# One GpSimd power for the RMS root, block 0 started by four heads, and a new written order: sliding-window attention with a SwiGLU feed-forward on one Trainium2 core

## The chip, the cores and the metric

The kernel runs on one core of a Trainium2 chip. The metric is the time of one execution on the device in microseconds (us); lower is better. A core has TensorE (PE, matmuls; PEld is its weight load), VectorE (DVE), ScalarE (ACT), GpSimd (POOL) and SyncE (SP). SP and ACT issue DMAs through hardware queues, POOL through a software queue. The eight banks of PSUM take what PE writes.

## What is computed

Four sequences of 768 tokens with 8 heads of 64 go through causal attention with a window of 128 keys and 4 sink keys that every query sees; then an RMS norm; then a SwiGLU feed-forward of 512 to 1536 to 512:

```python
keep = is_sink | ((rel >= 0) & (rel < 128))
scores = np.where(keep, q @ k.T / sqrt(64), -1e9)
a = softmax(scores); x = a @ v                       # 3072 rows of 512
xn = x / np.sqrt(np.mean(x * x, -1) + 1e-6) * rms_g
g = xn @ w_gate
out = (g * sigmoid(g) * (xn @ w_val)) @ w_out
```

## The kernel before

**Blocks and groups.** The 3072 rows are 24 blocks of 128 tokens, numbered 0 to 23, six to a sequence. The feed-forward takes groups of four blocks (512 rows), numbered 0 to 5.

**One block of attention.** q, k and v of a block are loaded (`load_bf16` L351, `load_v` L355, by POOL, which casts to bf16; each is one DMA of 256 KB read). Only q and k of block 0 come as fp32 through SP (`load_f32` L343) and are cast by ACT or DVE (`cast` L347). q and k are transposed: up to block 7 by PE and a copy out of PSUM (`pe_t` L441, `copy_t` L450), from block 8 on by a DMA on SP (`dma_t` L457). Keys stand on the partitions: the scores of a key block hold its own queries and the next block's (`scores` L474; `tri_scores` L551 leaves out the masked triangle; `scores_last` L492). In blocks 0 and 1 the mask is a matmul ahead of the scores (`mask_bias` L464); later masks are multiplied by DVE or selected by POOL (`tri_pool` L590). ACT takes exponentials. `av` (L602) multiplies by v, which has a column of ones for the denominators, in two halves of four heads. `normal` (L655, DVE) divides. `square` (L666, ACT) sums the squares of a row. `rms` (L674, DVE) adds 1e-6, takes the reciprocal root by a start from the bits and a polynomial, six one-column instructions, and multiplies the row by root and gain `gb` (L693). The result xr is transposed into xnt, by PE for blocks 0 to 7 (`pe_x`, `copy_x`), by a DMA on SP from block 8 on (`dma_x` L719).

**The feed-forward.** `mms` (L971) makes gate (g) and value (v) sums, 16 matmuls of 128x128 to a bank in group 0, 8 of 128x256 in groups 1 and 2, 4 of 128x512 later; `tanh`, `silu`, `hidden` (ACT, DVE, DVE) make hT; `project` (L1004) takes four matmuls of 128x512 at a time; ACT evacuates and SP stores.

**What sets the order.** Nothing is scheduled when the program is built. The kernel lists its steps (1077 before) with what each needs and gives, and `Plan.run` replays them in an order that is written out: for each engine a list of step numbers (`ORDER`), the interleaving of the engines (`TURNS`) and the PSUM banks (`BANKS`). Names like LOAD_LEAD, T_LEAD, GATE_FROM only add to the needs that `Plan.run` asserts; they put no wait into the program. Each engine runs its list strictly in order; waits come from the data. A load on POOL also waits for the landing of the load eight before it.

In what follows sN are the scores of block N, avN its two products with v, qN, kN, vN its loads or transposes, msN the sum of squares. Before, POOL's list begins (after each name, its place among the loads where it matters): q1, identity, bias, k1, v0, wg columns 0-1 (4th), q2, q3, v1, k2, wg 2-3 (9th), k3, wv 0-1 (11th), wv 2-3 (12th), v2, wg 4-5, wg 6-7, wv 6-7, wv 4-5, wg 8, 9, 10-11 (18th to 20th), wv 8, 10-11, 9 (21st to 23rd), q4, v3, k4, q5, q6, wo first half, k5, v4, wo second half, q7, v8, q8, v5, k6, k7, k8, v6, v7, q9, k9, v9, q10, k10, v10, q11, k11, v11, and so on by blocks.

SP's list has after the first loads: the transposes q8, q9, k8, k9, q10, one store, q11, k10, k11, q12, q13, k12, ...

Of the kernel before, what the change touches and what calls it, by code (L numbers as in the profile page):

```python
# [9 lines left out]
ALU = mybir.AluOpType  # L10
# [5 lines left out]
P = 128  # L16
# [3 lines left out]
C3 = -5.0 / 16.0  # L20
T1 = 2.5258847276
TP = T1 - 4.2
TQ = 7.0 / T1
# [66 lines left out]
""",  # L90
    "ACT": """
24 20 22 199 177 175 178 176 182 180 181 183 168 188 222 204-206 211 207 212 209 191 210
217 226 228 227 229 195 598 220 236 603 613 618 608 243 633 628 260 623 245 247 246 248
638 278 262 255 264-267 197 280 282 284 653 273 320 648 643 295 297 659 290 322 299 301
300 302 276 324 325 293 326 327 309 664 678 669 683 674 333 312 693 340 316 341 688 342
343 698 355-357 336 358 703 370 371 708 372 318 373 349 385 364 387 718 713 723 739 379
399 401 400 402 728 418 419 733 420 393 421 409 763 758 778 768 754 773 744 749 427 433
414 783 434-436 448 449 793 450 798 451 442 808 788 819 803 463-466 813 457 824 480 475
482 494 496 497 495 513 488 514 515 504 834 838 516 848 843 853 829 863 868 858 878 873
525 883 531-533 893 509 888 534 899 923 549-551 928 552 938 543 567-569 918 570 585 587  # L100
933 943 948 561 953 579 958 909 904 968 593 963 914 973 1008 1003 994 998 1013 1028 1023
989 1038 1018 1033 984 1053 1048 1043 979 1069 1059 1064 1072 1073
""",
    "DVE": """
# [13 lines left out]
""",  # L118
    "POOL": """
25 8 9 26-28 31 34 30 32 37 35 29 38 33 39 41 42 40 43 45 47 44 48 46 49 36 50 53 57 52  # L120
54 51 56 63 62 60 55 58 64 61 59 65-99 467 469 468 470 481 100 483 101-108 517 520 109
518 519 535 538 537 536 110 553 555 554 571 573 556 572 588 586 574
""",
    "SP": """
# [7 lines left out]
ASDDSDGDPDPSPDPPPPPGPPPGPDPGPPDDPGAGPPPPADGPPPPGPPSPDPSADPGSDPSPGAAAPAGPAPPDAPPGPPAPDPAP  # L132
PPPADPGPDAGPPDPPDGAPPGPAPPAGDPAPAPDGADAPDGPAPPPADPAGPDAPADAGPPPPAPADGAPADGPPPPPAPPDPGPPD
DPAGPDPAGPDPGAPDDGPDGPDADGDPDGPADADPGAADPGPGDPADGAPDPGADAPGADADPGDPAPPDAPPDADAPGDPPADAGP
AAGPAPDAPPDPADPDAPGDAPDDGDPAPGDPPGSAAPGADAPGDPDGPPPDAGDAPGDADPPGADPAGDSAPPAGASPADPADSADP
PPGADAPGPSADDPGASAPGDPGSAPPGDPSADGAPDASDAPPDADPAGPPSAAADPAADPADPDAPAGADPGADPPDAPPADDPDGS
PDAPASAGDPPAPAGDSPADAPADDPPAGSADPPDASDPAGPADPSDDPGAPDDPADAPDGSDPDGPAGAPADSAPPADSDPPDGPDS
PDAGASPAAPDASGDPADSPDSDPGSPPPDDPSDGPDADPAPADPSDPSPDPSPDDAPDPDAPADPADAPDADAPDPDPASAPDASAP
DSADPADPDPASAPASADPAPPDASDPDAPSDASPADPDADPDPDPDAPASAPPDASADPAGPDGPGDPDGAPDPDPDPDAPAAGPSA
DGPAASGPADSPAGDPPGDDPGPPDGPDAAGPPDAGADPAGPAAGDPADAGPGPDSPGDPDASGPDGAADSPDAPDSDPPDSPDAPDS  # L140
ADPDSAPPDSDPSDAPDASPADDPDPDPADAPAAPDASADPADSPGSDGPDGSPGPGPAPAPADPAPDADPADAPDAGAPDGPGPAAP
AAPPADGDPPDGPDGDGPPAAPDSPGDPGAGPDAPPDPDPDPDAADPADPDDPAPAADPSDPDPDDPAAPPSPDDPAAPDPPSPPDPA
PSDSDSPASDPDPPPAAPDDPDPDPPAAPSDPDPAPDDPDPPPPAAPDADPSDPAAPDPDPAAPDDPDPDAPADPDPDPDPPDPAAPD
SPSDPPPPPAAPSASSPAADS
"""
BANKS = """
0123456701234567012345645645635654353513714370432704614654154761061305147237235720165760
7615743764051726351402376152376015237653746573746574631547613547647136210735462047136524
7012473650241762350741602735410721356421305406354063420675134632745013274350174362507431
6542371607152374153275461237104573604156324175032407615342047562310462317460170414217326  # L150
5047314243270172316412040572153042573045
# [4 lines left out]
def kernel(  # L156
# [35 lines left out]
    F32_LOADS = ("ks0","qs0")  # L192
    GROW = "SP"
    CAST_DVE = 600
# [10 lines left out]
    GATE_FROM = 8  # L205
    LOAD_LEAD = 10
    LEAD_FROM = 10
    WARM = 56
    GATE_LEAD = 14
    T_LEAD = 4  # L210
# [9 lines left out]
    ld = ctx.enter_context(tc.tile_pool(name="ld", bufs=LD))  # L220
# [59 lines left out]
    dve(150, lambda: nc.vector.memset(ones, 1.0), gives=["ones"], prio=-96)  # L280
    if WARM:
        zeros = const.tile([P, P], BF16, name="zeros")
        dve(70, lambda: nc.vector.memset(zeros, 0.0), gives=["zeros"], prio=-99.6)
# [50 lines left out]
    for i in range(NS):  # L334
        sp(430, 2600, lambda i=i: load_sink(i), ["vsink1", "grow"], [("vsink", i)], -70 + i)
# [7 lines left out]
    def load_f32(name, src, g, eng):  # L343
        T["st", name, g] = opool.tile([P, H, D], FP32, name="stage", tag="osb")
        eng.dma_start(out=T["st", name, g], in_=block_of(src, g))

    def cast(name, g, copy):  # L347
        T[name, g] = ld.tile([P, H, D], BF16, name=name)
        copy(out=T[name, g], in_=T.pop(("st", name, g)))

    def load_bf16(name, src, g):  # L351
        T[name, g] = ld.tile([P, H, D], BF16, name=name)
        nc.gpsimd.dma_start(out=T[name, g], in_=block_of(src, g))  # L353
# [76 lines left out]
    def scale_gb():  # L430
        nc.scalar.mul(gb, BANK.pop(("gb",)), C3)
# [709 lines left out]
```

## Time and profile before

| | |
|---|---|
| three runs | 241.31, 242.18, 242.49 us |
| median | 242.18 us |
| profiled execution: span from its first to its last instruction | 241.9 us |
| TensorE clock granted | 1.00 throughout |
| ACT busy, POOL busy | 122.8, 89.2 us |
| software queue (q0): packets, share of the time of 16 DMA engines | 81760, 79.3% |

The profile is one execution; it has no time of its own beside its span, which lies 0.28 us under the median of the runs. A page's row of a group gives line, engine, operation, output and inputs, count, then busy time, mean of one in ns, and idle time before with what ended it. In a row of the timeline the first number is the start in us, the second the duration in us, and the brackets give the idle time ahead and its releaser.

### The profile page before, as it was taken

Reading aid. Unit: us, or ns where it says so; the run is one execution under the profiler, and the core shown is the slowest. Engines: PE = TensorE matmul, PEld = TensorE weight load, DVE = VectorE, ACT = ScalarE, POOL = GpSimd, SP = SyncE. Lnnn points to the kernel's source line nnn. Section 1 sums busy time; section 2 is a strip of 40 time slices with the busy share of each in tenths; the row PEclk is TensorE's granted clock in tenths of the full one; section 3 lists DMA queues with packets and bytes.
Section 4 is the critical chain, followed back from the end, with each engine's and each line's share of the span. In section 5 each row is a group of like instructions: output and inputs, shape, how many; then the busy total and the mean of one; then the engine's idle time right before and its main releaser. Section 6 shows DMA issues by size and latency. Waiting matters only on the chain.

```text
span 241.9 us, 5897 instructions
## 1 busy us (share of the span) xinstructions
PE 231.3 (96%) x2329; PEld 147.6 (61%) x2354; DVE 187.4 (77%) x478; ACT 122.8 (51%) x267; POOL 89.2 (37%) x116
## 2 busy tenths in 40 slices
PE   7889999999879999999999999999999999999995
PEld 5568986876668776777876644445554444444443
DVE  3599989989979999999898989994569946537520
ACT  4776368667766574337654464454543321233112
POOL 8985894597526554000004982022540000000000
PEclk9999999999999999999999999999999999999999
DMA  9999999999999999999601999527010114101024
GB/s 128 143 183 195 182 178 194 162 143 139 137 151 152 138 143 154 132 233 156 126 2 24 119 150 123 131 70 128 3 23 0 32 36 173 43 0 47 0 87 173
DMA packets 113741, 27.42 MB, mean 113 GB/s; under 512 B 103857, under 2 KB 110769, under 8 KB 113714
## 3 DMA queue, kind: packets, MB, share of 16 engines
q0 software_dynamic: 81760, 13.90, 79.3%
q1 hardware_dynamic: 31810, 12.95, 29.8%
q8 instruction: 18, 0.29, 0.5%
q10 hardware_dynamic: 144, 0.20, 0.2%
q14 instruction: 9, 0.07, 0.1%
HBM read 28.35 MB, written 6.29 MB: 143 GB/s over the span
## 4 chain that ended last, share of the span: by engine, by line
PE 67%; DMA 20%; POOL 6%; issue 2%; DVE 2%; SPq 2%; POOLq 0%
PE v L975 20%; PE o L1008 20%; PE g L975 18%; DMA wo<-in_moe_w_out_dram 5%; DMA qkT<-q 4%; DMA wv<-in_moe_w_val_dram 4%; DMA wg<-in_moe_w_gate_dram 3%; DMA q<-in_q_dram 3%; POOL v L357 2%; SPq L459 2%; PE s L563 2%; PE av L621 2%; POOL k L353 1%; PE av L616 1%; PE o_last L1028 1%
## 5 line engine op out<-in xcount | busy, mean ns | idle before, releaser
L975 PE MATMUL v<-xnt,wv 128*128 128x128 bf16 (+2 forms) x527 | 72.2, 282 | 0.4 <-DMA wv<-in_moe_w_val_dram 0.2
L975 PE MATMUL g<-xnt,wg 128*128 128x128 bf16 (+2 forms) x521 | 71.3, 281 | 0.4
L1008 PE MATMUL o<-wo,hT 128*128 128x512 bf16 x259 | 65.3, 379 | 1.1 <-issue 0.5
L982 ACT ACTIVATE th<-g 128x512 bf16<-128x512 f32 x72 | 41.7, 599 | 48.4 <-PE g L975 48.2
L988 DVE SCALAR_TENSOR_TENSOR p<-th,g 128x512 bf16<-128x512 bf16 x72 | 48.1, 682 | 18.9 <-ACT th L982 18.7
L975 PEld LDWEIGHTS <-wv 128*128 128x128 bf16 x528 | 43.3, 98 | 21.3 <-DMA wv<-in_moe_w_val_dram 0.6
L998 DVE TENSOR_TENSOR hT<-p,v 128x512 bf16<-128x512 bf16 x72 | 48.1, 682 | 9.3 <-PE v L975 7.8
L975 PEld LDWEIGHTS <-wg 128*128 128x128 bf16 x528 | 42.8, 98 | 19.3 <-issue 1.0
L1008 PEld LDWEIGHTS <-hT 128*128 128x128 bf16 x276 | 25.4, 98 | 26.5 <-issue 0.2
L597 POOL TENSOR_SCALAR_AFFINE_SELECT e<-e 128x512 bf16<-128x512 bf16 x20 | 12.7, 656 | 54.4 <-ACT e L572 53.0
L572 ACT ACTIVATE e<-s 128x384 bf16<-128x384 f32 x52 | 23.1, 495 | 12.5 <-PE s L563 12.5
L1016 ACT ACTIVATE osb<-o 128x512 f32<-128x512 f32 x23 | 13.4, 597 | 21.8 <-PE o L1008 18.0
L357 POOL DMA_DIRECT2D v<-in_v_dram x24 | 21.3, 888 | 8.5 <-DMA q<-in_q_dram 3.8
L353 POOL DMA_DIRECT2D q<-in_q_dram x23 | 20.4, 891 | 9.9 <-DMA k<-in_k_dram 6.7
L353 POOL DMA_DIRECT2D k<-in_k_dram x23 | 20.4, 889 | 9.1 <-DMA v<-in_v_dram 4.5
L669 ACT ACTIVATE sq<-x 128x512 bf16<-128x512 bf16 x24 | 15.1, 631 | 14.8 <-DVE x L661 14.5
L661 DVE TENSOR_TENSOR x<-av,rden 128x256 bf16<-128x256 f32 x48 | 20.4, 424 | 1.7
L693 DVE SCALAR_TENSOR_TENSOR xr<-x,r,gb 128x512 bf16<-128x512 bf16 x24 | 18.7, 778 | 0.8
L621 PE MATMUL av<-v,e 128*128 128x65 bf16 x192 | 16.4, 193 | 0.3 <-DMA v<-in_v_dram 0.3
L536 ACT ACTIVATE e<-s 128x512 bf16<-128x512 f32 (+1 forms) x36 | 15.1, 519 | 1.6 <-PE s L485 1.5
L616 PE MATMUL av<-v,e 128*128 128x65 bf16 x160 | 14.8, 193 | 0.0
L621 PEld LDWEIGHTS <-e 128*128 128x128 bf16 x192 | 12.7, 97 | 2.8 <-DVE e L547 0.4
(78 smaller groups left out, 192.6 us busy)
## 6 DMA issues: line engine op xcount, KB each, us to landing
out_dram<-osb SPq DMA_DIRECT2D x23, 256.0 KB, 2.2
v<-in_v_dram POOLq DMA_DIRECT2D x24, 128.0 KB, 8.9
q<-in_q_dram POOLq DMA_DIRECT2D x23, 128.0 KB, 8.1
k<-in_k_dram POOLq DMA_DIRECT2D x23, 128.0 KB, 9.6
wo<-in_moe_w_out_dram POOLq DMA_DIRECT2D x2, 768.0 KB, 11.3
wg<-in_moe_w_gate_dram POOLq DMA_DIRECT2D x5, 256.0 KB, 8.0
wv<-in_moe_w_val_dram POOLq DMA_DIRECT2D x5, 256.0 KB, 8.9
stage<-in_k_dram SPq DMA_DIRECT2D x1, 256.0 KB, 3.0
```

Source lines behind the costliest of these rows:

```text
L353: nc.gpsimd.dma_start(out=T[name, g], in_=block_of(src, g))
L357: nc.gpsimd.dma_start(out=V16[b][:, t, :, 0:D], in_=block_of(v, g))
L572: nc.scalar.activation(out=e_tile(g)[:, x:x + 2, 0:TW], in_=BANK.pop(("s", g, u, hi))[:, 0:2 * TW].rearrange("p (j c) -> p j c", c=TW), fu ...
L616: nc.tensor.matmul(out=dest, lhsT=T["e", g - 1][:, x, P:2 * P], rhs=V16[b][:, t - 1, h, :], start=(t == 1), stop=False, skip_group_check=True,
L621: nc.tensor.matmul(out=dest, lhsT=T["e", g][:, x, 0:P], rhs=V16[b][:, t, h, :], start=(t == 0), stop=True, skip_group_check=True,)
L661: nc.vector.tensor_tensor(out=T["x16", g][:, 4 * u:4 * u + 4, :], in0=pvv[:, :, 0:D], in1=rden.unsqueeze(2).to_broadcast((P, 4, D)), op=AL ...
L693: nc.vector.scalar_tensor_tensor(out=T["xr", g], in0=T.pop(("x16", g)).rearrange("p h d -> p (h d)"), scalar=r[:, 3:4], in1=gb, op0=ALU.mu ...
L975: nc.tensor.matmul(out=ps[:, i * n:(i + 1) * n], lhsT=w_sb[:, kt, ft * P:(ft + 1) * P], rhs=T["xnt", G][:, kt, cols], start=(kt == 0), sto ...
L982: nc.scalar.activation(out=T["th", key], in_=BANK[("g", key)], func=ACT.Tanh, scale=0.5,)
L988: nc.vector.scalar_tensor_tensor(out=T["p1", key], in0=T.pop(("th", key)), scalar=1.0, in1=BANK.pop(("g", key)), op0=ALU.add, op1=ALU.mult,)
L998: nc.vector.tensor_tensor(out=T[hk][:, i:i + n, cols], in0=T.pop(("p1", key)).rearrange("p (n c) -> p n c", n=n), in1=BANK.pop(("v", key)) ...
L1008: nc.tensor.matmul(out=BANK[("o", G, tb)], lhsT=T["h", G, ft // 4][:, ft % 4, tb * P:(tb + 1) * P], rhs=wo[:, ft, :], start=(ft == 0), sto ...
```

## The change

**The root.** The square's sum gets four constant columns (two of 131*2^-13, two of 139*2^-18) whose squares stand for epsilon, in a tile that keeps x of three blocks; the root is one power -0.5 on GpSimd; DVE keeps only the scaling.

```diff
+    xall = const.tile([P, 3, DM + 4], BF16, name="xall")
+    nhalf = const.tile([P, 1], FP32, name="nhalf")
...
+    def eps_columns():
+        for i, c in enumerate((131 * 2.0 ** -13, 139 * 2.0 ** -18)):
+            nc.vector.memset(xall[:, :, DM + 2 * i:DM + 2 * i + 2], c)
+        nc.vector.memset(nhalf, -0.5)
...
-            T["x16", g] = xpool.tile([P, H, D], BF16, name="x16")
+            T["x16", g] = xall[:, g % 3, 0:DM].rearrange("p (h d) -> p h d", h=H)
...
+    def root(g):
+        r = T["rs", g] = small.tile([P, 1], FP32, name="r")
+        nc.gpsimd.tensor_tensor(
+            out=r, in0=T.pop(("ms", g)), in1=nhalf, op=ALU.pow,
+        )
...
     def rms(g):
-        m = small.tile([P, 1], FP32, name="m")
-        nc.vector.tensor_scalar(
-            out=m, in0=T.pop(("ms", g)), scalar1=1e-6, scalar2=None, op0=ALU.add,
-        )
...
-        for o, i0, s0, s1, op0 in (
-            (0, y, y, m, ALU.mult), (1, r[:, 0:1], -T1, y, ALU.add),
-            (2, r[:, 0:1], TP, r[:, 0:1], ALU.add), (3, r[:, 2:3], TQ, r[:, 1:2], ALU.add),
-        ):
-            nc.vector.tensor_scalar(
-                out=r[:, o:o + 1], in0=i0, scalar1=s0, scalar2=s1, op0=op0, op1=ALU.mult,
-            )
         T["xr", g] = xpool.tile([P, DM], BF16, name="xr")
         nc.vector.scalar_tensor_tensor(
-            out=T["xr", g], in0=T.pop(("x16", g)).rearrange("p h d -> p (h d)"),
-            scalar=r[:, 3:4], in1=gb, op0=ALU.mult, op1=ALU.mult,
+            out=T["xr", g], in0=xall[:, g % 3, 0:DM],
+            scalar=T.pop(("rs", g)), in1=gb, op0=ALU.mult, op1=ALU.mult,
         )
```

`gb` is copied where it was multiplied by a constant of the polynomial.

**Block 0 by four heads.** k and q of block 0 come in halves of four heads, k's by SP, q's by ACT; each half is cast, transposed (two transposes), copied and scored against its own queries separately. The mask matmul of block 0 is cut likewise: first for its own queries, later for the next block's.

```diff
-    for i, name in enumerate(F32_LOADS):
+    for i, (n, u, e) in enumerate((("k", 0, "SP"), ("q", 0, "ACT"), ("k", 1, "SP"), ("q", 1, "ACT"))):
...
+    def pe_t_half(n, u):
+        ps = bank((n, 0, u)).bitcast(BF16)
+        for i in range(2):
+            nc.tensor.transpose(
+                out=ps[:, i * P:(i + 1) * P],
+                in_=T[n, 0][:, HP * u + 2 * i:HP * u + 2 * i + 2, :], identity=ident,
+            )
...
+        if g == 0:
+            for u in range(2):
+                pe(110, lambda u=u: scores(0, 0, 1, (u,)),
```

The clearing of the sink keys' tile of the first two sequences is a step of its own, early; the four loads of v's sink rows no longer name the gain's load among their needs. The extra needs (LOAD_LEAD, T_LEAD, the gates from block 8) are dropped.

**The order.** All lists are new up to about the start of group 4 on PE, ACT and DVE, and throughout on POOL; SP's list is the same but for the first loads. POOL's list now begins, rsN being the power of block N: q1, k1, bias, identity, v0, q2, v1, wg 2-3 (6th), k2, q3, wv 2-3 (9th), wg 0-1 (10th), wv 0-1 (11th), wg 6-7 (12th), wg 4-5 (13th), rs0, v2, wv 6-7, wv 4-5, q4, rs1, k3, q5, wg 9 (20th), k4, wg 8 (22nd), wg 10-11 (23rd), rs2, v3, wv 9, 8, 10-11 (25th to 27th), k5, q6, wo first half, v4, rs3, v5, k6, q7, wo second half, q8, k7, v6, rs4, v7, rs5, k8, q9, q10, k9, k11, q12, rs6, v8, k10, q11, q14, v10, v9, rs7, q13, ...

PE's list, warm-up matmuls left out (g and u are gate and value sums with group, first column, first row; p a projection with group, block, part; x the transposes of xr):

```
before: mask0 k0 q0 q1 s0(own) s0(next) gain av0 k1 av0 mask1 q2 s1 s1 q3 k2 av1 x0 av1 sinks s2
        g000 u000 k3 x1 av2 av2 g0.0.128 g040 u0.0.128 g0.4.128 x2 u040 ...
        ... p020 p000 k5 p010 x3 s5 av4 g0.8.384 av4 g0.4.384 q6 g0.0.384 q7 p001 u0.4.384 av5 p002 av5
        k6 u0.8.384 u0.0.384 k7 s6 p011 x4 p012 s7 p030 x5 av6 p031 av6 g120 p021 g100 av7 av7 p022 p032
        u100 x6 g160 s8 sinks g140 u120 g180 s9 ...
after:  k0a mask0 q0a k0b q0b s0a(own) s0b(own) q1 k1 gain s0(next) av0 q2 av0 mask1 s1 s1 k2 q3 av1 x0 av1
        s2 sinks g000 x1 u000 g0.0.128 g0.4.128 av2 av2 u0.0.128 g040 u040 q4 x2 u0.4.128 k3 ...
        ... s5 sinks g0.4.384 g0.0.384 g0.8.384 u0.8.384 av4 u0.4.384 p020 u0.0.384 q7 av4 k6 av5 av5
        p000 p030 p001 p002 s6 p021 x5 k7 p022 x4 p031 p032 s7 g100 av6 p010 av6 p011 u100 g120 g160 av7
        p012 sinks s8 g140 av7 u120 x6 g180 s9 u160 u140 av8 av8 g1.10.0 u180 x7 u1.10.0 g1.0.256 s10 ...
```

More of the change, by code (lines that the diff above doesn't have):

```diff
@@ L341, in block_of, with half, load_f32, cast @@
         return src[b, :, t * P:(t + 1) * P, :].rearrange("h t d -> t h d")
[L343 to L349, printed above, removed]
+    def half(u):
+        return slice(u * HP, (u + 1) * HP)
+    def load_f32(name, src, g, u, eng):
+        if ("st", name, g) not in T:
+            T["st", name, g] = opool.tile([P, H, D], FP32, name="stage", tag="osb")
+        eng.dma_start(
+            out=T["st", name, g][:, half(u), :], in_=block_of(src, g)[:, half(u), :])
+    def cast(name, g, u, copy):
+        if (name, g) not in T:
+            T[name, g] = ld.tile([P, H, D], BF16, name=name, tag=f"{name}{g % LD}")
+        copy(out=T[name, g][:, half(u), :], in_=T["st", name, g][:, half(u), :])
     def load_bf16(name, src, g):
-        T[name, g] = ld.tile([P, H, D], BF16, name=name)
+        T[name, g] = ld.tile([P, H, D], BF16, name=name, tag=f"{name}{g % LD}")
         nc.gpsimd.dma_start(out=T[name, g], in_=block_of(src, g))
@@ L462, in dma_t, with mask_bias, scores @@
         )
-    def mask_bias(g):
+    def mask_bias(g, n0=0, n1=2):
         for u in range(2):
             for hi in range(2):
+                slot = ("s", g, u, hi)
+                if slot not in BANK:
+                    bank(slot)
                 nc.tensor.matmul(
-                    out=bank(("s", g, u, hi)), lhsT=ident if g % NT else idnos,
-                    rhs=bias.rearrange("p n c -> p (n c)").unsqueeze(1).to_broadcast(
-                        (P, 2, 2 * P)),
+                    out=BANK[slot].rearrange("p (j c) -> p j c", j=2)[:, :, n0 * P:n1 * P],
+                    lhsT=ident if g % NT else idnos,
+                    rhs=bias.rearrange("p n c -> p (n c)")[:, n0 * P:n1 * P].unsqueeze(1).to_broadcast(
+                        (P, 2, (n1 - n0) * P)),
                     start=True, stop=False, skip_group_check=True,
                 )
-    def scores(g, n0, n1):
+    def scores(g, n0, n1, us=(0, 1)):
         b, t = divmod(g, NT)
         qkT = T["qkT", b]
-        for u in range(2):
+        for u in us:
             for j in range(2):
@@ L782, in block_scores @@
         parts = [(0, 1), (1, 2)] if g in SPLIT else [(0, nq)]
-        if g < PE_MASKS:
+        if g == 0:
+            pe(430, lambda: mask_bias(0, 0, 1), [("bias", 0), "idnos"], [("mb", 0)], pa,
+               takes=slots)
+        elif g < PE_MASKS:
             pe(864, lambda g=g: mask_bias(g), [("bias", 0), ("bias", 1), "ident", "idnos"]
                + ([("qp", g), ("kp", g)] if g else []), [("mb", g)], pa, takes=slots)
+        if g == 0:
+            for u in range(2):
+                pe(110, lambda u=u: scores(0, 0, 1, (u,)),
+                   [("kT", 0, u), ("qT", 0, u), ("mb", 0)] + ([("s", 0, 0, 0)] if u else []),
+                   [("s", 0, 0, u)] + ([("s", 0, 0)] if u else []), pa + 1, mode=1)
+                for hi in range(2):
+                    act(270, lambda u=u, hi=hi: exps(0, u, hi, 0, 1, False),
+                        [("s", 0, 0, u), "table"] + ([("x", 0, u, 0, 0)] if hi else []),
+                        [("x", 0, u, hi, 0)], early)
+            parts = parts[1:]
         for n0, n1 in parts:
@@ L789, in block_scores @@
             needs += [("s", g, 0)] if n0 else []
+            needs += [("x", 0, u, hi, 0) for u in range(2) for hi in range(2)] if g == 0 else []
             needs += [("mb", g)] if g < PE_MASKS else []
@@ L882 @@
         for n in "qk":
-            if g < QK_DMA_FROM:
+            if g == 0:
+                for u in range(2):
+                    pe(115, lambda n=n, u=u: pe_t_half(n, u), [(n, 0, u), "ident"],
+                       [(n + "p", 0, u)], pa, takes=[(n, 0, u)])
+                    ways = {"DVE": (200, lambda n=n, u=u: copy_t_half(n, u, nc.vector.tensor_copy)),
+                            "ACT": (300, lambda n=n, u=u: copy_t_half(n, u, nc.scalar.copy))}
+                    either(ways, [(n + "p", 0, u), "table"] + ([(n + "T", 0, 0)] if u else []),
+                           [(n + "T", 0, u)] + ([(n + "T", 0)] if u else []), early,
+                           drops=[(n, 0, u)])
+            elif g < QK_DMA_FROM:
                 pe(225, lambda n=n, g=g: pe_t(n, g), [(n, g), "ident"] + old, [(n + "p", g)],
@@ L934 @@
         act(720, lambda g=g: square(g),
-            [("n", g, 0), ("n", g, 1), "table"] + ([("ms", g - 1)] if g else []), [("ms", g)],
+            [("n", g, 0), ("n", g, 1), "table", "eps"] + ([("ms", g - 1)] if g else []), [("ms", g)],
             early)
-        dve(1745, lambda g=g: rms(g),
-            [("ms", g), "gb"] + ([("xt", g - 3)] if g >= 3 else [])
+        pool(570, lambda g=g: root(g), [("ms", g)], [("rs", g)], early, mode=9)
+        dve(700, lambda g=g: rms(g),
+            [("rs", g), "gb"] + ([("xt", g - 3)] if g >= 3 else [])
             + ([("xr", g - 1)] if g else []), [("xr", g)], early, mode=9)
```

126 lines of the change are left out of this document (61 added, 65 removed), and 75 rows, old and new, of the table ORDER.

## Prediction

> **What bounds the kernel now.** I read the page's first two parts, then TensorE's waits, then the timeline of each engine in the first 65 us, then the chain.
>
> ```profile
> span 241.9 us, 5897 instructions
> PE 231.3 (96%) x2329; PEld 147.6 (61%) x2354; DVE 187.4 (77%) x478; ACT 122.8 (51%) x267; POOL 89.2 (37%) x116
> ...
> PE s L563 <- DMA qkT<-q: 1.3, 1, 1.3
> PE s L563 <- DMA qkT<-k: 0.8, 1, 0.8
> ```
>
> PE is busy for 231.3 of 241.9 us. The waits (us in total, times, longest) show no wait of PE for DVE after its first instruction but one of 0.2 us for a mask, and after 20 us only two over 0.4 us: the scores of blocks 8 and 9 (s8 at 65.68, s9 at 70.49) wait for transposes of q and k by DMA, 2.1 us together. So a gain can come from two places: these 2.1 us, and the first 20 us, where PE runs warm-up matmuls and short pieces.
>
> The first 20 us are paced by loads. POOL issues them, and from the ninth on each issue waits for the landing of the one eight before it:
>
> ```profile
> 15.46 0.74 POOL L399 DMA_DIRECT2D wv<-in_moe_w_val_dram  x1 [0.27 <-DMA wg<-in_moe_w_gate_dram]
> ...
> 18.98 0.74 POOL L399 DMA_DIRECT2D wg<-in_moe_w_gate_dram  x1 [0.57 <-DMA wv<-in_moe_w_val_dram]
> ...
> 30.36 0.88 POOL L353 DMA_DIRECT2D k<-in_k_dram  x1 [0.37 <-DMA wv<-in_moe_w_val_dram]
> ```
>
> These are loads 17, 20 and 30; they show loads 9, 12 and 22 landing just before 15.5, 19.0 and 30.4. Thirteen loads in 14.9 us is 1.15 us each. The chain has the same two stretches: POOL's issues and weight loads, then one q load and a transpose:
>
> ```profile
> 12.86 8.02 DMA wg<-in_moe_w_gate_dram
> ...
> 59.75 10.61 DMA qkT<-q
> ```
>
> **The change, part by part.** *The root.* Six one-column DVE instructions go. In the timeline of DVE they begin at 11.75 and the scaling at 13.05:
>
> ```profile
> 11.75 0.14 DVE L676 TENSOR_SCALAR m<-ms 128x1 f32<-128x1 f32 x1
> ...
> 13.05 0.75 DVE L693 SCALAR_TENSOR_TENSOR xr<-x,r,gb 128x512 bf16<-128x512 bf16 x1
> ```
>
> That is 1.30 us a block, 31 us in all, 17% of DVE's busy time. As PE does not wait for DVE, I count this as nothing by itself. One POOL power is added per block. No row shows one: bounds are 0.10 us (POOL's one-column memset) and 0.85 us (the longest 128x512 select); I take 0.65, the median of those selects, since a power is a long routine on little data; the low end would bring each later load 0.5 us forward. The four extra columns of the square add 4/512 of 0.63 us, 5 ns a block, on an engine that is half idle: nothing. The scaling of gb only becomes a copy.
>
> *The power's place.* It stands in POOL's queue among the loads. It waits for the square of its block, and all loads behind it wait too. This is the part that counts, below.
>
> *The halves of block 0.* k and q come in four pieces of 128 KB over two queues (SP and ACT) instead of two of 256 KB over SP. The bytes are the same; before, the two landed at 3.85 and 4.75. ACT's two issues (about 0.5 each, as on SP) push its table load (1.28, from 0.80) to end at 3.1, ahead of its first cast: nothing. If the first pair lands at 3.4, the DVE casts (0.35 each by half the ACT cast of 0.62), the half transposes and copies (0.26 for half of 0.42 with its fixed part), both masks and two score groups put the first exponential at about 7.1, against 7.31. But the second half of block 0's scores now stands ahead of its first av, behind k1's transpose (k1 lands about 6.8 by its 4.5 us), and its other av stands behind q2's transpose (about 10.4). So the sum of squares comes at about 13.3, not 11.2, the root at 13.9, xr at 14.75 (before 13.80), and xnt's first quarter at 15.2 to 15.6 (before 15.38). The half start is worth nothing by itself, and costs nothing as long as the first gate matmul (16.60) waits for something else: in the new load order wg's first columns are load 10, so 16.4 to 16.6.
>
> *The new load order.* The first value matmuls need loads 11 and 12 before, 9 and 11 after: one load less, 1.15 us. Gate columns 4 to 7 move from places 14 and 15 to 12 and 13. Columns 8 to 11 move later (gate 18-20 to 20-23, value 21-23 to 25-27), but their matmuls are moved back by as much: at 1.15 us a load, value columns are complete at 35.5, and PE reaches them at 35.3 by my count of its list (0.9 us for each 16 matmuls of 128x128). I take **1.1 us gained**; the bounds are 0 (every just-in-time load late by 1.1) and 2.0 (the remaining warm-up and short waits also close). Nothing is gained after that by order alone, as PE is dense: 4.6 to 5.0 of each 5 us between 20 and 65 us.
>
> *Blocks 8 to 10.* Before, block 5's av ended at 50.3. In the new list four projections (0.86 each) come after it instead of ahead, and two value groups (0.88) ahead: 50.3-3.4+1.7-1.1 = 47.5. Then normalizing 0.8, square 0.9, root 0.65: 49.9. Only now POOL may issue k8 (0.88) and q9 (begins 50.8); before these began at about 41.7 and 47.27. From 47.5 to s8 the list has 11 projections (9.5), four gate or value groups (3.5) and 2.5 of small pieces: s8 is reached at 63.0, s9 2.6 later, s10 at 72.9.
>
> How long a load and a transpose take depends on what is in flight. The loads right after POOL's long pause landed 3.9 (k, 133.3), 4.5 (v, 134.8) and 6.6 us (q, 135.6) after issue; in the crowded 47 to 62 us, 7.1 to 16. Transposes landed in 6.9 to 10.6 us there, in 2.4 to 3.7 once the loads had stopped, and in 5.9 when one started at 135.9 among fresh loads. In the changed kernel each root makes such a pause. So q9, second after a pause, lands at 55.3; SP transposes it (1.2), then k8 at 56.5, then k9 and q10 (59.1). With 5.9 all are there by 62.4 and 65.0: s8 and s9 do not wait, **2.1 us gained**. Then q11 stands behind the root of block 6: av6 ends at 57.4, its root at 60.1; v8 and k10 go first, q11 begins at 62.4, is third after the pause (6.6) and lands at 69.0; its transpose 1.3, k10's begins at 70.3 and takes between 3.5 (the row at 145.4) and 5.9; I take 4.3: 74.6, and s10 waits **1.7 us**, a new wait. Bounds for s8 to s10: no wait at all (2.1 gained), or 5.8 at s8 and 1.8 more at s10 (loads of 7.3 and transposes of 9.5 us, crowded rows; 7.6 lost). Later blocks have 8 us and more between transpose and scores up to block 19, as before, or fall in the quiet part.
>
> Sum: 241.9-1.1-2.1+1.7 = 240.4 for the span. The median of the three runs shown is 242.18, 0.28 above the profiled span, so **240.7** for the time. About 0.5% (1.2 us) is what a measurement of this kernel can tell from no change.
>
> **The rivals.** *Crowded transposes (slower).* The loads held by roots 5 and 6 come late, and the transposes land as slowly as before. At 7.3 and 9.5 us s8 and s10 wait 7.6 us: 241.9-1.1-2.1+7.6+0.3 = 246.6; halfway to the forecast, 243.6. Both gains are eaten when k10's transpose takes 5.8 us (70.3+5.8-72.9 = 3.2), and from 7 us on it is slower by over 0.5%. For it: every transpose between 47 and 104 us took 6.9 us or more. Against: in the 16 us from q9's issue 13 loads are issued, not 16, with a gap among them.
>
> *The start brings nothing, or the gain goes at s10 (same).* With 5.9 for k10's transpose s10 waits 3.3 and the sum is 0.1 above the old; with the start's 1.1 lost it is 241.8. For it: half of the early weights arrive within 1 us of their use by my count. Time 241.2 to 242.8.
>
> *The power has a dear first call (slower).* The first power would hold POOL by some 6 us at 13.3, and with it xr, the first gate matmuls and every load behind: PE would start dense work about 5 us late, 246.9. Against: in this trace the two pool configurations take 33 and 37 ns at 2.3 us, and the select behind them runs at 2.42 for 0.30 us, the second for 0.29: no first call is dearer. The 6 us are what the Trainium skill, GPSIMD Engine Reference, section Instruction dispatch, gives for the first call of a freshly loaded routine ("approximately 6 µs", with no visible instruction); the trace does not agree for the select, and no run here shows it for a power.
>
> **How the numbers follow.** Forecast 0.52; crowded transposes 0.21; nothing gained 0.22; dear first call 0.05. The forecast's own range is 238.7 (no wait at s8 to s10) to 241.0. Faster is the first case; same the third; slower the second and fourth. For 8 in 10 the range runs from 238.6, through the third case, up to 245.0, which leaves out the upper part of the crowded case, the fourth, and a start better by 2.
>
> **What would show it.** Right: DVE about 31 us less busy; POOL powers near 0.65 us; the first value matmuls done about 1 us earlier; no PE wait at s8 and s9, one of 1 to 3 us at s10 on a transpose. Wrong: PE waiting over 2 us at s8 (crowded); a POOL gap of several us at the first power; PE waits for weights between 17 and 36 us (start lost); first exponentials well before 7 us, or roots early enough that POOL never stands still for one, would make it faster than I say.

## The result

The changed kernel takes 244.59 us (median of six runs, 243.97 to 245.84); the kernel before took 242.01 beside it (241.11 to 242.49). The ratio is 1.0123, with a 95% interval of 1.0097 to 1.0149: slower by 1.2%. The forecast was 240.7 and faster: the time lies in its range, but the kernel moved the other way. Medians here and below are of all runs; the intervals leave out three runs (one each of e7, e8 and e13) that took over 1.5% longer than their kernel's fastest.

Every later record holds both a run's time and its span, and the time is 1.7 us longer than the span, before the change and after. The first profile of before (span 241.9) was therefore an execution of about 243.6 us, longer than any run listed with it. A second profile of the kernel before, at 241.55 us, has a span of 239.8; it is the one to compare with (e1 below), and the loss of span is 242.7 - 239.8 = 2.9 us.

### The profile page after: what moved, and what is told of

Read it like the earlier page. It is cut to its first block, busy times and chain, and to the rows that moved or that the text cites. A ratio compares the mean times of both kernels' runs of the same rounds, so it can differ in the third digit from the quotient of the medians.

```text
span 242.7 us, 5814 instructions
## 1 busy us (share of the span) xinstructions
PE 230.6 (95%) x2332; PEld 147.6 (61%) x2358; DVE 165.3 (68%) x346; ACT 119.1 (49%) x262; POOL 103.8 (43%) x140
## 4 chain that ended last, share of the span: by engine, by line
PE 72%; DMA 13%; DVE 5%; POOL 3%; issue 3%; ACT 2%; SPq 0%; DVEq 0%; POOLq 0%
PE o L1056 20%; PE v L1023 20%; PE g L1023 20%; DMA qkT<-k 6%; DMA q<-in_q_dram 4%; PE av L645 2%; DMA xnt<-xr 2%; PE s L587 2%; PE av L640 2%; DMA stage<-in_q_dram 1%; ACT sq L693 1%; POOL r L700 1%; PE o_last L1076 1%; PE s L509 1%; POOL v L364 1%
## 5 line engine op out<-in xcount | busy, mean ns | idle before, releaser
L1056 PE MATMUL o<-wo,hT 128*128 128x512 bf16 x260 | 64.6, 379 | 1.0 <-issue 0.3
L1036 DVE SCALAR_TENSOR_TENSOR p<-th,g 128x512 bf16<-128x512 bf16 x72 | 48.6, 686 | 21.4 <-ACT th L1030 21.0
L1023 PEld LDWEIGHTS <-wg 128*128 128x128 bf16 x528 | 42.3, 98 | 19.4 <-issue 1.5
L700 POOL TENSOR_TENSOR r<-ms,nhalf 128x1 f32<-128x1 f32 x24 | 14.0, 583 | 64.0 <-ACT sq L693 63.9
L706 DVE SCALAR_TENSOR_TENSOR xr<-xall,r,gb 128x512 bf16<-128x512 bf16 x24 | 18.4, 765 | 4.9 <-POOL r L700 4.9
L693 ACT ACTIVATE sq<-xall 128x516 bf16<-128x516 bf16 x24 | 15.4, 640 | 12.6 <-DVE xall L685 12.5
L685 DVE TENSOR_TENSOR xall<-av,rden 128x256 bf16<-128x256 f32 x48 | 20.4, 425 | 1.7
L560 ACT ACTIVATE e<-s 128x512 bf16<-128x512 f32 (+1 forms) x36 | 15.8, 512 | 6.9 <-PE s L509 6.2
L684 DVE RECIPROCAL rden<-av 128x4 f32<-128x4 f32 x48 | 8.5, 177 | 15.3 <-PE av L645 15.1
L645 PE MATMUL av<-v,e 128*128 128x65 bf16 x192 | 17.1, 193 | 0.2 <-ACT e L560 0.2
```

Of the source, the lines that this page charges most:

```text
L645: nc.tensor.matmul(out=dest, lhsT=T["e", g][:, x, 0:P], rhs=V16[b][:, t, h, :], start=(t == 0), stop=True, skip_group_check=True,)
L685: nc.vector.tensor_tensor(out=T["x16", g][:, 4 * u:4 * u + 4, :], in0=pvv[:, :, 0:D], in1=rden.unsqueeze(2).to_broadcast((P, 4, D)), op=AL ...
L693: nc.scalar.activation(out=sq, in_=xall[:, g % 3, :], func=ACT.Square, scale=1.0 / math.sqrt(DM), accum_out=T["ms", g],)
L706: nc.vector.scalar_tensor_tensor(out=T["xr", g], in0=xall[:, g % 3, 0:DM], scalar=T.pop(("rs", g)), in1=gb, op0=ALU.mult, op1=ALU.mult,)
L1023: nc.tensor.matmul(out=ps[:, i * n:(i + 1) * n], lhsT=w_sb[:, kt, ft * P:(ft + 1) * P], rhs=T["xnt", G][:, kt, cols], start=(kt == 0), sto ...
L1036: nc.vector.scalar_tensor_tensor(out=T["p1", key], in0=T.pop(("th", key)), scalar=1.0, in1=BANK.pop(("g", key)), op0=ALU.add, op1=ALU.mult,)
```

## The profile after

The head of the page, then TensorE's waits (us in total, times, longest):

```profile
span 242.7 us, 5814 instructions
PE 230.6 (95%) x2332; PEld 147.6 (61%) x2358; DVE 165.3 (68%) x346; ACT 119.1 (49%) x262; POOL 103.8 (43%) x140
```

```profile
PE x L721 <- DVE xr L706: 1.9, 2, 1.6
PE s L587 <- DMA qkT<-k: 1.8, 2, 1.3
...
PE k L459 <- DVE k L356: 0.7, 1, 0.7
PE g L1023 <- DMA xnt<-xr: 0.4, 1, 0.4
PE s L490 <- DVE idnos L306: 0.4, 1, 0.4
```

DVE is 22 us less busy, and PE waits more. s8 (64.87) and s9 (68.53) do not wait; s10 (76.54) waits 1.3 us for k10's transpose, s16 0.5, block 1's transposes 1.6 for xr1. Where the time went is read from PE's busy time in the same stretches of both (start and end, length, busy time and matmuls, clock, DMA share, GB/s). The second profile of before:

```profile
0.00:20.00 20.00, 16.44 (x196) 1.00 1.58 158
20.00:45.00 25.00, 24.74 (x425) 1.00 1.74 185
...
65.00:80.00 15.00, 14.95 (x235) 1.00 1.98 153
80.00:100.00 20.00, 19.84 (x192) 1.00 2.00 144
100.00:130.00 30.00, 29.74 (x359) 1.00 0.83 118
```

After:

```profile
0.00:20.00 20.00, 15.32 (x182) 1.00 1.52 157
20.00:45.00 25.00, 24.82 (x465) 1.00 1.79 169
...
65.00:80.00 15.00, 13.70 (x228) 1.00 1.83 151
80.00:100.00 20.00, 19.46 (x210) 1.00 1.50 126
100.00:130.00 30.00, 29.12 (x322) 1.00 1.23 143
```

Length less busy time is PE's idle time: 1.12 us more in the first 20 us, 1.25 more from 65 to 80, 0.38 and 0.62 more in the next two, and 0.47 more behind 200 us; the other stretches differ by 0.16 or less. In all PE idles 3.5 us more, and as it is counted busy for 0.6 us less (230.6 against 231.2), the span grows by 2.9. Most of the loss is thus a worse start and waits for transposes.

POOL's timeline shows the powers among the loads (brackets: idle time ahead and its releaser):

```profile
14.51 0.56 POOL L700 TENSOR_TENSOR r<-ms,nhalf 128x1 f32<-128x1 f32 x1 [1.79 <-ACT sq L693]
...
49.98 0.56 POOL L700 TENSOR_TENSOR r<-ms,nhalf 128x1 f32<-128x1 f32 x1 [6.24 <-ACT sq L693]
...
52.01 0.78 POOL L700 TENSOR_TENSOR r<-ms,nhalf 128x1 f32<-128x1 f32 x1 [0.58 <-ACT sq L693]
52.75 0.91 POOL L360 DMA_DIRECT2D k<-in_k_dram  x1
...
61.71 0.56 POOL L700 TENSOR_TENSOR r<-ms,nhalf 128x1 f32<-128x1 f32 x1 [3.66 <-ACT sq L693]
```

A power takes 0.58 us on average, the first one 0.56. POOL stood still 63.9 us ahead of powers, 6.24 of it ahead of block 4's, with v7, block 5's power, k8 and q9 behind. The chain shows how such a pause reaches PE around s16 (start, duration, what):

```profile
104.84 1.76 POOL v L364 x2
106.60 4.39 issue
111.03 0.57 POOL r L700
111.60 0.87 POOL k L360
112.47 3.01 DMA q<-in_q_dram
115.47 8.49 DMA qkT<-k
```

POOL waits 4.39 us for block 13's square; k19, q18, q19 and two v go out behind its power; among these fresh loads a transpose of k takes 8.49 us, and s16 starts behind it at 124.01.

## The experiments

The theories: L, the powers hold loads, transposes come late and PE waits. S, the new start of block 0 costs, because its square is late. D, what DVE sheds is what the new order lives on. H, the halves cost. M and W came later: M, the mask matmuls' new place at the start costs; W, PE's clock comes up late in some executions, because PE has gaps at the start. Times are medians; the ratio is to runs of the kernel before on the same chip (241.77 to 241.94).

| kernel | us | ratio, 95% interval | span |
|---|---|---|---|
| e1 before again | 241.54 | 0.9994 [0.9979, 1.0009] | 239.8 |
| e2 after, polynomial root on DVE | 258.30 | 1.0679 [1.0639, 1.0719] | 257.4 |
| e3 before, power on GpSimd | 240.80 | 0.9962 [0.9932, 0.9991] | 238.9 |
| e4 after, casts by ACT | 246.66 | 1.0205 [1.0133, 1.0277] | 245.5 |
| e5 after, loads ahead of powers | 243.47 | 1.0063 [1.0040, 1.0086] | 241.8 |
| e6 after, block 0's square earlier | 245.48 | 1.0155 [1.0116, 1.0193] | 243.0 |
| e7 e5 and e6 together | 244.14 | 1.0087 [1.0053, 1.0120] | 240.8 |
| e8 after, block 0 whole | 249.22 | 1.0281 [1.0243, 1.0320] | 247.5 |
| e9 after, masks early | 244.76 | 1.0122 [1.0091, 1.0152] | 243.4 |
| e10 e7 and e9 | 243.31 | 1.0075 [1.0051, 1.0100] | 242.3 |
| e11 e7, more warm-ups | 242.53 | 1.0030 [1.0010, 1.0051] | 240.9 |
| e12 e3, power behind some loads | 241.60 | 0.9999 [0.9985, 1.0012] | 240.0 |
| e13 after, more warm-ups | 243.56 | 1.0070 [1.0041, 1.0099] | 241.8 |
| e14 e5, more warm-ups | 242.54 | 1.0034 [1.0010, 1.0058] | 240.3 |
| e15 e11, block 0 whole | 243.59 | 1.0069 [1.0045, 1.0093] | 242.5 |
| e16 e3, more warm-ups | 240.80 | 0.9965 [0.9947, 0.9984] | 239.0 |

**e1: the kernel before, unchanged.**

> The kernel before, unchanged, to read its times and spans side by side. The changed kernel's time lies 1.7 us above its span in every run (244.37 and 242.7 in the profiled one), while its span is only 0.8 us longer than that of before (241.9). Theory O (the loss lies outside the span): this run's time lies about 0.1 us above its span, so 1.6 us of the 2.6 lost lie outside the span, around the first and last instruction. Theory I (the loss is inside): its time lies 1.7 us above its span too, its span is near 240.3, and the execution first shown was a long one for this kernel.

The waits that the forecast meant to win, 2.1 us at s8 and s9, are 0.2 us in this execution:

```profile
PE s L563 <- DMA qkT<-k: 0.2, 1, 0.2
```

**e2: the changed kernel with the polynomial root on DVE, nothing on POOL.**

> The changed kernel with the old polynomial root back on DVE (five one-column instructions per block, epsilon still in the columns, gain row scaled as before) and nothing on POOL; all orders as in the changed kernel. Theory L (the roots in POOL's queue hold the loads, so transposes come late): POOL no longer stops, the scores of block 10 do not wait, and the time falls by 1.5 to 2.5 us to 242 to 243, although DVE is 27 us busier. Theory S (the loss is made at the start, by block 0's halves and the order of its pieces): the first gate matmul stays at 17.4 and the time at 244 to 245. Theory D (DVE's relief is worth something): slower than the changed kernel, 246 or more.

13.7 us slower than the change. DVE is as busy as before (187.3 us), and now PE waits for it all along. (Each of the four executions also lists a mean clock of 0.993; in the profile it is 0.50 from 23.3 to 26.7 us.)

```profile
PE x L735 <- DVE xr L720: 5.4, 5, 2.1
...
PE s L593 <- DVE xall L691: 1.2, 2, 0.7
PE o L1070 <- DVE xall L691: 1.1, 2, 0.9
```

D is right: the new order counts on a short DVE. It says nothing on what the power is worth elsewhere.

**e3: the old order, with epsilon columns and the power right behind each square.**

```diff
 def square(g):
     ...
+        r = T["rs", g] = small.tile([P, 1], FP32, name="r")
+        nc.gpsimd.tensor_tensor(
+            out=r, in0=T.pop(("ms", g)), in1=nhalf, op=ALU.pow,
+        )
     ...
 def rms(g):
-    ...   (six one-column instructions)
```

> The kernel before with one part alone: epsilon columns and the power on POOL, placed behind the square in the written order; all loads and orders as before. Theory L: in this order the loads stand ahead of most roots, so POOL stops little after 40 us; but roots 0 to 2 now stand among the weight loads and may hold them; time 241.5 to 243.5, near the kernel before. Theory S: the power is harmless, 241 to 242. A power that is dear in itself would show 245.

Faster than before by 0.4%. DVE's busy time falls from 187.1 to 163.6 us. So the power by itself does not make the kernel slow; the split start and the new orders, with the power's place in them, do, by 3.8 us against this kernel. POOL stands still ahead of powers for 55.1 us here too: that alone costs nothing.

**e4: block 0's casts on DVE go to ACT.**

> The changed kernel with the three half casts that DVE did moved to ACT, orders unchanged. In its trace two of DVE's casts took 0.72 us and a third 0.27, the long ones while POOL was issuing a load, and the copy of the mask's identity 0.57 where it took 0.26 before. Theory P (DVE's copies from one buffer to another are held while POOL writes a load's descriptors): ACT casts take 0.40 each whatever POOL does, the first transposed half comes 0.3 us earlier or equal, and the time falls by up to 0.5 us. Rival (the casts are off the path, k1's landing sets the start): first gate matmul and time unchanged, 244 to 245.

The first exponential comes 0.4 us earlier (7.82), block 1's transposes 0.05 (20.07), and then more is lost from 65 to 130 us (PE waits 1.9 us for xnt, 1.7 for DVE). Slower than either outcome that was expected. The casts do not bound the start. Why the later waits grew is not settled.

**e5: 21 loads (the text on record says 25) put ahead of the powers of blocks 4 to 13.**

```diff
-POOL: ... k7 v6 rs4 v7 rs5 k8 q9 q10 k9 k11 q12 rs6 v8 k10 q11 q14 v10 v9 rs7 ...
+POOL: ... k7 v6 k8 q9 q10 k9 rs4 v7 rs5 k11 q12 k10 q11 v8 rs6 q14 v10 v9 q13 k12 rs7 ...
```

> The changed kernel; POOL's list alone is altered: 25 loads that stood behind the powers of blocks 4 to 13 (k8, q9, q10, k9 behind that of block 4; k10, q11, v8 behind block 6; and so on up to k19, q18, q19, v17, v15 behind block 13) stand ahead of them. Theory L (the powers hold the loads behind them, transposes come late, PE waits): PE's idle time between 65 and 130 us, 2.72 us in the changed kernel and 0.47 in the kernel before, falls to 1 us or less, s10 starts near 75.2 instead of 76.54, and the time goes to about 242.9 from 244.6. Theory S (only the start of block 0 costs): the waits go or move but the time stays within 0.5 of 244.6. A third outcome: more loads in flight at once make transposes slower, and the time rises above 245.

1.1 us faster than the change, and the intervals do not meet. PE's idle time from 65 to 130 us is gone, though POOL still stands still for 62.5 us ahead of powers: what counts is which loads stand behind them. But s7 now waits for q8's transpose, which has more loads beside it:

```profile
45.00:65.00 20.00, 18.66 (x207) 1.00 1.94 145
65.00:80.00 15.00, 15.00 (x245) 1.00 2.06 149
80.00:100.00 20.00, 20.00 (x215) 1.00 1.36 121
100.00:130.00 30.00, 30.00 (x337) 1.00 1.22 140
```

```profile
PE s L588 <- DMA qkT<-q: 1.3, 1, 1.3
```

L is right in mechanism; about half of what it removes comes back as the third outcome.

**e6: block 0's av, square and scaling earlier; the first value matmuls ahead of block 1's transposes.**

> The changed kernel; in the first 20 us alone: block 0's products with v stand ahead of its scores for the next block, its square ahead of the second four exponentials, its scaling ahead of a copy of k2, the gain's matmul behind those scores, and the first value matmuls ahead of the transposes of block 1. Theory S (the start costs 1.1 us of PE's time because block 0's square comes 2.5 us later than before and the transposes of block 1 wait 1.6 us): first root near 12.8 instead of 14.5, first gate matmul at 16.6 instead of 17.45 (wg's first columns), first value matmul at 17.7 instead of 20.36, no 1.6 us wait, PE idle of the first 20 us 3.6 instead of 4.68, time about 243.5. Theory L: the first 20 us may improve, but the waits between 65 and 130 us take it back, and the time stays within 0.5 of 244.6.

Not faster. **e7, both edits:**

> Both edits together. If L and S are both right and add up: 244.6 - 1.7 - 1.1 = 241.8, that is the kernel before again or a little under. If one takes back what the other gives: 243 or more. Under 240.8 (what the kernel before with the power alone took) it would be the best kernel so far, and the halves and orders would be worth something once these two places are mended.

No gain over e5 in the median, though its profiled run took 242.52; but for one run of 246.83, the runs lie between 242.28 and 245.90. Profiles of e6 and e7 have the same instructions up to 9 us, yet the first scores stand at 7.89 and 7.26. TensorE's rows, e6 first:

```profile
5.86 1.03 PE L491 MATMUL s<-bias,idnos 128*128 128x256 bf16 x4 [0.16 <-DVE idnos L307]
...
7.89 0.40 PE L510 MATMUL s<-qkT 64*128 64x128 bf16 x4
```

```profile
5.86 0.61 PE L491 MATMUL s<-bias,idnos 128*128 128x256 bf16 x4 [0.38 <-DVE idnos L307]
...
7.26 0.29 PE L510 MATMUL s<-qkT 64*128 64x128 bf16 x4
```

The same four matmuls take 1.03 and 0.61 us: in e6 the array still runs at about half speed, until about 10 us, and block 0's transposes come 1.17 us later (17.07 and 15.90). At the first projection e6 is still 1.17 us behind (46.93 and 45.76). Hence theory W.

**e8: block 0's k and q whole, in the same order of steps.**

```diff
 def load_f32(name, src, g, u, eng):
     ...
-        eng.dma_start(
-            out=T["st", name, g][:, half(u), :], in_=block_of(src, g)[:, half(u), :])
+        if u == 0:
+            eng.dma_start(out=T["st", name, g], in_=block_of(src, g))
```

(casts, transposes and copies likewise)

> The changed kernel with k and q of block 0 whole again (k by SP, q by ACT, one cast, four transposes and one copy each), in the same order of steps; the scores keep their halves. Theory H (the halves themselves cost, by long casts on DVE and a late first half): first exponential at 7.8 or earlier instead of 8.23, and the time about 0.5 to 1 us lower, 243.8. Theory S (the order of the steps costs, the halves are worth nothing): first exponential 8.0 to 8.6, first root within 0.3 of 14.5, time within 0.5 of 244.6.

4.6 us slower: H is wrong for this way of loading whole blocks, against which the halves help. (Both whole over SP in turn, as before the change, was not tried in the new order; in e1 they land 2.9 and 3.4 us after issue.) The whole loads over two queues land 4.1 and 4.7 us after issue, the halves 3.2 and 3.9. That makes the start 1 us later; the rest is in waits of 2.3 us (q's transpose), 1.6 (xnt) and a clock of 0.94 between 100 and 130 us in the profiled run.

**e9: identity and pattern ahead of k1's load, block 0's whole mask ahead of the first transposes.**

> The changed kernel; in the first 6 us alone: identity and mask pattern are built on POOL ahead of the load of k1 (as before the change), and block 0's whole mask matmul (512 columns a bank) is put ahead of the first transposes, while PE still waits for k and q. Theory M: the split start costs because the mask work, which lay in PE's free time before (3.3 to 5.2 us), now lies behind the casts (0.61 us at 5.86 and 0.61 at 10.39), and because PE stands idle from 4.42 to 5.08 and from 5.36 to 5.86, so that its full speed comes at 5.1 in some executions and only at about 7.6 in others (the two profiles with first scores at 7.26 and at 7.89). Then first scores come at 6.5 to 7.0 in every execution, and the time goes to about 243.5 from 244.6. Theory O (only the order from 9 us on costs): first scores earlier by 0.5, first root still near 14.2, time within 0.5 of 244.6.

The time is O's, the way there neither's: first scores stay at 7.25, block 0's transposes come 0.4 us earlier (15.52 against 15.92), and PE then waits 2.9 us for k's transposes instead of 1.8: what the start gains, L takes.

**e10: this with the two edits of e7.**

> The three edits together (loads ahead of the powers, block 0's products and square earlier, masks early). Theory M and L add: 244.14 (the first two together) less about 0.8: 243.3, and the spread of the runs, 4.6 us there, shrinks to 2.5. If the halves and the new order are worth anything, this is where it shows: at or under 240.8. Otherwise it stays over 242.

243.31 is the number forecast for M and L, but by luck: first scores stay at 7.26, where M has them at 6.5 to 7.0. The spread is 2.8. Its profile shows the clock itself (stretches of 1 us; the clock stands behind the brackets):

```profile
11.00:12.00 1.00, 1.00 (x4) 1.00 2.29 149
12.00:13.00 1.00, 1.00 (x10) 0.54 1.82 154
...
15.00:16.00 1.00, 1.00 (x19) 0.75 1.47 195
```

PE was idle 0.51 us of the two between 9 and 11; from 12.1 to 15.5 it runs at half clock, and block 0's transposes come at 17.00, 1.1 us late. Six of the eleven executions list a mean clock of 0.991 to 0.993, as this one does; they take 243.98 us on average, the other five 243.02. Such a fall thus costs about 1 us here, as far as eleven runs can tell.

**e11: e7 and nine more warm-up matmuls.**

```diff
-        nc.tensor.matmul(out=ps[:, 0:P], lhsT=zeros, rhs=zeros, start=True, stop=True)
+        for _ in range({0: 3, 43: 3, 6: 3, 32: 3, 31: 2}.get(i, 1)):
+            nc.tensor.matmul(out=ps[:, 0:P], lhsT=zeros, rhs=zeros, start=True, stop=True)
```

> The first two edits together and nine more warm-up matmuls of 128x128, six ahead of the first transposes and three behind: PE busy without a gap from 1.46 to 5.08 and nearly to 5.86. Theory W (the spread is the state of PE's clock at the start: executions in which full speed comes at 7.6 instead of 5.1 are 1.2 us longer): the median falls from 244.14 to about 243.3 and the slow executions thin out; first scores at 7.26. Rival (the spread comes from the transfers): median and spread stay within 0.5.

1.6 us less than e7, spread 2.05 instead of 3.62 (e7 without its longest run). That is W's outcome and a little more, but it does not show W's cause: the profile's first scores stand at 7.32, and two executions still list a clock of 0.991 and 0.992. The records kept with the traces tell when full speed begins: between 4.4 and 6.1 us in the profiles of the change, e4, e5, e7, e9 and e10, at 8.9 in e8, 9.7 in e2 and 9.9 in e6; with the added warm-ups between 4.4 and 7.0 (e11, e13, e14, e15). Three late ones of nine against none of four point W's way and are too few to prove it.

**e12: the power behind the loads that stand between square and scaling, in the old order.**

> The kernel before with epsilon columns and the power on GpSimd (240.80 with the power right behind the square), the power now where the scaling stands in the written order, that is behind the loads written between square and scaling: one load for blocks 0, 2, 3, 4, 6, 8, two or more for 5 and 9 to 11. Theory L: loads go earlier, the first value matmul at 18.1 instead of 18.94, and the time is 240.3 to 240.8, below the kernel before. Rival: the power and with it the scaling come later by up to 1.7 us and PE waits for xr: 241.5 or more.

0.8 us over e3, though the intervals overlap. The rival is right: PE waits 0.7 us for xr, and the loads of the old order needed no help. The first value matmul comes at 17.65, but not by the power's place: e16, with the power right behind the square, has it at 17.55. The 18.94 of e3's profile is that of its one execution with a window of half clock.

**e13, e14, e15: what each part is worth with the warm-ups.**

> The changed kernel with the nine more warm-up matmuls alone. Theory W (part of the loss is PE's clock: with PE idle from 4.42 to 5.08 and 5.36 to 5.86 us, some executions run a window of about 3.4 us of the start at half clock, 1.1 to 1.2 us each): the median falls from 244.6 to about 243.5. Rival (the 1.6 us that the warm-ups gave beside the other two edits came from elsewhere): within 0.5 of 244.6.

> Loads ahead of the powers and the warm-ups, without the earlier square of block 0. Against 242.53 with all three edits, this tells what the earlier square is worth: theory S (the late square costs): 243.3 or more. If the square's place is worth nothing (x1 waits for its root as long in both): 242.5 or less, and the loss of the start is the clock and the split itself.

> All three edits, with k and q of block 0 whole. With the transfers' waits and the clock mended, this is the worth of the halves alone: theory H0 (they are worth nothing): 242.53 plus or minus 0.5. Theory H+ (a whole pair that comes over two queues at once lands at 4.9 and 5.5 us, halves at 4.1 and 4.7, so halves are worth 0.8): 243.3. If it comes near 247, the halves matter by a mechanism that I have not seen.

e13: 1.0 us under the change, as W says. But the profiles of both start alike (first scores 7.26 and 7.27); they part at s10, which does not wait in e13's, as q11 landed 0.6 us sooner. All executions of the change and of e5 list a clock of 0.997 or more, so a fall as in e10 is not what the warm-ups mend there; a late first rise, which these lists don't show, is left. That the clock makes this 1.0 us is thus inferred, not seen. e14 equals e11 (242.54 and 242.53): the earlier square is worth nothing, S in that form is wrong. e15 is 1.06 over e11, with intervals that overlap by a hair: with the other places mended the halves are worth about 1 us against whole loads over two queues, H+. So most of e8's 4.6 us came of something else, the clock and the transposes by its profile; which part of which is open.

**e16: six more warm-ups in e3.**

> The kernel before with the power right behind the square (240.80) and six more warm-up matmuls between 5.9 and 7.7 us, where PE stood idle 0.45 us ahead of a window of 3.1 us at half clock (9.9 to 13.0 in its profile). Theory W: no such window, first gate matmul at 16.6 instead of 17.64, median 240.0 or less: the best of all. Rival: that window lies in the shadow of the loads, and the median stays within 0.4 of 240.8.

240.80 again: the rival's outcome, but a weak test. The first gate matmul comes at 16.08 instead of 17.64 in the profiles; yet of e3's ten executions only the profiled one lists a low clock (0.992, the others 0.999 or more), so its median had little to gain. That one took 240.65, under the median, which speaks for the rival. In the old order mask matmuls fill PE from 3.3 to 5.2 us. e3 and e16 are the best versions, 0.4% under the kernel before.

**The account.** Against e3 the changed kernel loses 3.8 us. The warm-ups give back 1.0 of it and the moved loads 1.0 more (e14); 1.7 are left. From s20 to the last matmul e14 and e16 take the same time (136.53 to 236.92, 135.62 to 236.01: 100.39 each), so the 0.9 us by which their last matmuls differ arise before; 0.35 of it is more idle time of PE in the first 20 us, 0.33 in the next 25. Another 0.35 lies behind the last matmul (spans of 240.3 and 239.0). Where the rest of the 1.7 is, these profiles don't show.

## Why the prediction was wrong, step by step

- **The base.** "These 2.1 us" at s8 and s9 were taken from one execution about 2 us longer than the median, as a standing loss. e1 shows 0.2. This is the step that fails first: without it the forecast's own sum was 239.8 - 1.1 + 1.7 = 240.4 against 239.8, that is no change or a little slower. The step from span to time, 0.28, has the same fault: each run lies 1.7 over its own span, so a span of 240.4 meant a time of 242.1, where the kernel before already was.
- **The new load order, 1.1 us gained: wrong.** The first value matmul came at 20.36, not about 1 us before 18.1, and PE idled 1.12 us more in the first 20 us. In the new list this matmul stands behind the transposes of xr1, which waited 1.6 us for the chain of blocks 0 and 1. The step took each load's place for its matmul's time. With the value matmuls put ahead of them (18.55 in e7's profile) the median did not fall below e5's either.
- **The halves.** "Worth nothing by itself, and costs nothing": the second is wrong. First exponential at 8.23 (forecast 7.1), sum of squares done at 14.43 (13.3), root at 15.07 (13.9), first gate matmul at 17.45 (16.4 to 16.6). q's first half landed at 4.1 instead of 3.4, identity stood behind k1's load (3.57 instead of 2.42), two DVE casts took 0.72 and 0.73 instead of 0.35, and the mask matmul left the free time before the loads. Against whole loads over two queues the halves gain about 1 us (e15); against the loads of the kernel before they were not measured alone, so the first stays open.
- **The wait at s10: right**, 1.3 us against 1.7, by the mechanism forecast, though q11's load was issued 1.6 us and s10 reached 2.3 us later than it says. Missing were the same pauses behind the powers of later blocks (s16, xnt), which the prediction put at nothing.
- **The power's price: right**, 0.58 us against 0.65. No dear first call: 0.56. The Trainium skill (GPSIMD Engine Reference, Instruction dispatch) gives about 6 us for a freshly loaded routine; this trace does not agree for this one.
- **DVE 31 us less busy:** 23.5 in e3. 1.30 us a block is from start to start; some 4 us of the difference are DVE's pauses between these instructions (0.8 to 0.9 us in each of five groups of e1), the rest was not taken apart. "I count this as nothing by itself" does not hold: the new order is written for the short DVE (e2), and in the old order the power gave 1.1 us.
- **The rivals.** By its time, 244.6 falls to the first, but by luck: s8 was to wait there, and it doesn't. By its mechanism the second is nearest, whose start brings nothing. None named PE's clock.

## What to carry to other kernels

Take the base of a sum from an execution at the median, and count a wait as winnable only if a second profile shows it. An operation that waits, put into an engine's queue among loads, delays each load behind it; whether that costs is decided by the slack of the load's consumer, so look at it block by block (in e3 POOL stands still for 55 us at no cost). Who moves away work that filled TensorE before the first data arrive should try something in its place: nine warm-up matmuls gave 1.0 to 1.6 us in the new order, six gave nothing in the old one.

## What the runs showed of the hardware

**The clock's window.** In e10 and e3 the granted clock falls to 0.50 for 3.4 us (12.1 to 15.5; 9.7 to 13.1) and returns by itself, after stretches of 1 us in which PE was busy for 55 to 91%. The Trainium skill (TensorE: Matmul & The Clock Gate, Part 1) tells of a free-running window of 3413 ns; the length agrees. It puts the fall after an idle window; here it came without one: of the 3.41 us ahead PE was busy for 2.74 in e3 and 2.91 in e10. The changed kernel was busy for only 1.78 us from 18.4 to 21.8 and kept 1.00, so PE's idle share as the profile counts it does not tell when the clock falls; what does is open. The half speed of e6's start doesn't stand in the clock column (1.00): it is read from the rows' durations.

**DVE copies beside a load's issue.** DVE's timeline after, while POOL issues loads without a pause:

```profile
4.12 0.72 DVE L356 CAST q<-stage 128x256 bf16<-128x256 f32 x1 [2.26 <-DMA stage<-in_q_dram]
4.75 0.27 DVE L356 CAST k<-stage 128x256 bf16<-128x256 f32 x1
...
5.05 0.57 DVE L305 COPY idnos<-ident 128x128 bf16<-128x128 bf16 x1
...
5.87 0.73 DVE L356 CAST k<-stage 128x256 bf16<-128x256 f32 x1
```

The same cast takes 0.27 or 0.72 us, the copy 0.57 (0.26 before, where it ran beside POOL's building of the mask pattern). POOL's issues run from 3.82 to 4.72, to 5.61 and to 6.48; the long copy ends with the second, the long casts 0.12 us after the first and the third. The Trainium skill (SBUF — State Buffer, Who interferes with whom) says that a DVE copy or cast in a mode that uses both ports and a GpSimd instruction lock a shared port pair for a whole instruction; the long durations agree. The short cast does not: it lies inside the second issue (4.75 to 5.02). What part of an issue holds a copy is thus not shown.
